# Making a second set of left operands late, in place, instead of storing it and reading it back, and adding two of four kinds of block sums by DMA

## The chip, the core and the metric

The kernel runs on one core of a Trainium2 chip. The engines named in the text are PE (TensorE, the matrix engine; PEld is its weight load), DVE (VectorE), ACT (ScalarE), POOL (GpSimd) and SP (SyncE). In this kernel SP only issues plain DMAs, and POOL issues the other DMAs: the stores and all accumulating ones. All DMAs of the core share 16 DMA engines. The metric is the device time of one execution in microseconds, the median of three runs.

## The reference

With x of 2048 x 512, the reference computes y = g * A + (1 - g) * B, where

- g = sigmoid(sum over d of x * gate_w), one value for a row
- A = Cr @ (x @ Hr^T) - Ci @ (x @ Hi^T): the real part of a two-dimensional Fourier transform, with the matrices Hr, Hi (512 x 512) and Cr, Ci (2048 x 2048) given as inputs
- B = (relu(x @ Wg) * (x @ Wu)) @ Wd, with a hidden width of 1792

```
a = jnp.einsum("bsd,ed->bse", x, dft_hid_re)
b = jnp.einsum("bsd,ed->bse", x, dft_hid_im)
y = jnp.einsum("ts,bse->bte", dft_seq_re, a) - jnp.einsum("ts,bse->bte", dft_seq_im, b)
gate = jnp.einsum("bsd,df->bsf", x, W_gate); up = jnp.einsum("bsd,df->bsf", x, W_up)
b = jnp.einsum("bsf,fd->bsd", gate * (gate > 0) * up, W_down)
return g * a + (1 - g) * b
```

All of it is in float32.

## The kernel before, in words

**Products.** A float32 operand is split into two float32r parts: hi is a copy of it on ACT, lo is operand minus hi on DVE. A product is then three passes over PE: lo*hi, hi*lo, hi*hi. On top of that each matrix product of two by two blocks is done with seven block products instead of eight (Strassen's way, in Winograd's form). Each of the seven needs a left and a right operand that is a block or a sum of blocks. They are numbered 1 to 7; for the stages looked at here they run in the order 1, 5, 6, 3, 7, 2, 4.

**Stages.** In order of time: the blocks of the gated unit (relu and product, the result h goes to DRAM as hd); two spectral parts, which compute x @ Hr^T and x @ Hi^T and store them to DRAM as ad; two more blocks of the gated unit; two Down rounds (h @ Wd; the result goes to vd, its negative to zd); four Sequence rounds, numbered here by (m, p): m = 0 is Cr, m = 1 is Ci, p is one half of the output rows. They run (0,0), (0,1), (1,1), (1,0); the last is of the class `Last`.

**A Sequence round** has 7 products x 4 groups (jj) of 12 matmuls = 336 matmuls of 128 x 128 by 512. The left operands are the spectral result, one set of 14 tiles of 512 KB in hi and lo (28 tiles) for each m; the right ones are blocks "11", "12", "22", "21" of Cr or Ci, 512 KB for each block and jj, loaded by SP into tiles `r`. Sums of blocks are made in place (`rights`, line 850): for product 5, r11 += r12; for 7, r12 += r22; for 6, r11 += r22; for 4, r11 += r21. Before the change all four kinds are DVE additions, four of each in a round. Each right operand is split into `ch` (ACT) and `cl` (DVE), 31 and 24 matmuls ahead of its use by the plan. When a product is done, `evac` takes PSUM out with ACT or DVE, and `done` brings a finished block of the output on its way: with m = 0 it is added to zd by an accumulating DMA.

**Left operands.** The class `Left` (line 700) loads the four blocks of ad as `l`, makes the sums 5, 7, 6 and 3 on DVE, and splits each into `lh` and `ll`. The set of m = 0 is made during Down 1 and round (0,0) and stays in SBUF. The set of m = 1 is made early by `prep` (line 733), one half (n = 0) during the second spectral part and one (n = 1) during Down 0; its 28 tiles are stored to a DRAM tensor `lb` by POOL, and `fetch` (line 746) reads them back with SP during round (0,1), each as soon as the tile of the first set that it replaces is used up.

**The last round.** `Last.prepare` (line 883) runs during (1,1): for all four blocks it loads z from zd and v from vd, makes v + gate * z on DVE and stores it to vd by POOL. In (1,0) the blocks "12" and "22" then take vd by an accumulating DMA (line 894), and "11" and "21" load v again and add the product's two halves on DVE.

**What sets the order.** Nothing is scheduled by hand. Each operation is handed to a planner (`Plan`, line 128) with a key, the number of the matmul beside which it may start. The planner models the durations of all engines and one common line for DMA data, works out how late each operation may be, and writes one fixed order for each engine. ACT and DVE may run up to 40 matmuls ahead of a key, SP and POOL not at all. SBUF is 51 units of 4 KB for each partition; a load or a result waits in the plan until a unit is free, and on the chip until the last user of its unit is done, a storing DMA included. Every engine, SP and POOL too, works through its order strictly in turn. Two constants of the model concern DMAs: the time of its data (line 111) and `LANDING` (line 133).

```
op(key + 18, lambda t=t, m=m, x=x: store(to[m - 1, n, x], f32(t.all)))
for x, (o, i) in {5: ("11", "12"), 7: ("12", "22"), 6: ("11", "22"), 4: ("11", "21")}.items():
    op(at[x, jj] - SUM[x], lambda r=r, o=o, i=i: combine(r[o].all, r[o].all, r[i].all, 1))
op(k + 10, lambda b=b, v=v: store(vd[self.place(b)], v.all))
```

Of the kernel before, what the change touches and what calls it, by code (L numbers as in the profile page):

```python
# [9 lines left out]
F32R = mybir.dt.float32r  # L10
# [4 lines left out]
P = 128  # L15
# [73 lines left out]
class Step:  # L89


    def __init__(self, key, engine, name, a, k):
        self.key, self.engine, self.name, self.a, self.k = key, engine, name, a, k
        refs = [x for x in a if isinstance(x, Ref)]
        refs += [k[x] for x in ("out", "in_") if isinstance(k.get(x), Ref)]
        writes = [k["out"] if "out" in k else a[0]]
        if "accum_out" in k:
            writes.append(k["accum_out"])
        self.writes = [x for x in writes if isinstance(x, Ref)]
        self.reads = [x for x in refs if x is not writes[0]]  # L100
        if "accum_op" in k or name == "matmul" and not k["start"]:
            self.reads += self.writes
        self.after, self.start, self.end, self.due = set(), None, None, None
        n = writes[0].size() if self.writes else 0
        self.hold = None
        if name == "tensor_copy":
            self.work = 0.1 + n * 0.52e-3
            self.hold = self.work - 0.05
        elif name == "dma_start":
            n = max(x.size() // (P if x.base.kind == "dram" else 1) for x in (*self.writes, *self.reads))  # L110
            self.work = n * 4 * P / 4096 * 0.157 / 16 * (2 if "accum_op" in k else 1)
        elif engine == "tensor":
            self.work = self.hold = 0.22667 * n / N
        elif engine == "vector":
            self.work = 0.16 + n * 1.0417e-3
            self.hold = self.work - 0.083
        else:
            self.work = 0.19 + n * 0.845e-3
            self.hold = self.work - 0.09
# [8 lines left out]
class Plan:  # L128
# [1 line left out]

    MATMUL, WAIT, LANDING = 0.22667, 0.035, 2.1

    ISSUE = {"sync": 0.5, "scalar": 0.5, "gpsimd": 0.9}

# [6 lines left out]
    def op(self, key, f, *a):  # L143
        self.ops.append((key, len(self.ops), f, a))
# [133 lines left out]
def kernel(ctx: ExitStack, tc, xP, xG, wf, wgu, wd, cr, ci, wri, gw, out):  # L278
# [27 lines left out]
    def hbm(name, *shape):  # L306
        return Buf(plan, name, shape, kind="dram", tile=dram.tile(list(shape), F32, name=name))
# [1 line left out]
    hd = hbm("hd", 2, 7, P, KF // 2, N)  # L309
    ad = hbm("ad", 2, 2, 2, 2, P, 4, HD)  # L310
    vd, zd = (hbm(n, NT, P, KD, N) for n in ("vd", "zd"))
    lb = hbm("lb", 7, 2, 2, P, 4, HD)
    wb = hbm("wb", 8, P, 4, 2, P)
    gd = hbm("gd", NT * KD, P)
    gwt = Buf(plan, "gwt", [D], kind="fixed", tile=small.tile([P, D], F32, name="gwt"))
# [5 lines left out]
    def buf(name, shape=(2, N), dtype=F32):  # L321
        return Buf(plan, name, list(shape), dtype)
# [21 lines left out]
    def E():  # L344
        return plan
# [4 lines left out]
    def f32(ap):  # L350
        return ap.bitcast(F32)
# [4 lines left out]
    def load(o, i):  # L356
        plan.sync.dma_start(o, i)

    def store(o, i):
        plan.gpsimd.dma_start(out=o, in_=i)  # L360
# [42 lines left out]
    class Weights:  # L403
# [34 lines left out]
        def fetch(self, key):  # L438
            for n, t in enumerate(y for x in (self.a, self.b) for i in x for y in i):
                k = t.shape[0]  # L440
                op(key + 6 * n, lambda n=n, t=t, k=k: load(f32(t.all), wb[n, :, :k]))
# [182 lines left out]
    class Spectral:  # L624
# [8 lines left out]
        def prep(self, m, key):  # L633
            raw = self.raw[{1: "11", 2: "12", 4: "22", 7: "21"}[m]] if m in (1, 2, 4, 7) else buf(f"vs{m}")
            w = self.w[m] = buf(f"vh{m}", dtype=F32R), buf(f"vl{m}", dtype=F32R), raw
            if len(LEFT[m]) > 1:
                a, b = ((self.raw[n] if isinstance(n, str) else self.w[n][2]) for n in LEFT[m][:2])
                op(key, lambda: combine(raw.all, a.all, b.all, LEFT[m][2]))
            op(key + 4, hi_of, w)
            op(key + 8, lo_of, w)  # L640
# [59 lines left out]
    class Left:  # L700
# [29 lines left out]
                op(key, lambda: E().scalar.copy(hi[:, s], raw[:, s]))  # L730
                op(key + step, lambda: E().vector.tensor_sub(lo[:, s], raw[:, s], f32(hi[:, s])))

        def prep(self, n, key, step, to=None):

            for b in BLOCKS:
                op(key - 60, self.load, b, n)
            for m in (1, 5, 7, 6, 2, 3, 4):
                if m in (3, 5, 6, 7):
                    op(key, self.sum, m, n)
                self.split(m, n, key + 4, 8)  # L740
                for x in range(2):
                    t = self.t[m, n][x]
                    op(key + 18, lambda t=t, m=m, x=x: store(to[m - 1, n, x], f32(t.all)))
                key += step

        def fetch(self, m, n, key, of):
            t = self.t[m, n] = [buf(f"lb{m}", [4, HD], F32R) for _ in range(2)]
            for x in range(2):
                op(key, lambda x=x: load(f32(t[x].all), of[m - 1, n, x]))

    SUM = {5: 40, 7: 40, 6: 40, 4: 88}

    class Round:

# [86 lines left out]
    class Sequence(Round):  # L841
        HI, LO = 31, 24

        def __init__(self, left, m, p):
            self.m, self.p = m, p
            if m:
                self.g = gate_row(p, plan.now + 100)
            super().__init__(left, (2, 2, 2, 2))

        def rights(self):  # L850
            at = self.at
            for jj in range(4):
                r = {b: buf(f"r{b}") for b in BLOCKS}
                for b, key in (("11", at[1, jj]), ("12", at[5, jj]), ("22", at[6, jj] - 10), ("21", at[2, jj] - 36)):
                    op(key - 90, lambda r=r, b=b, jj=jj: load(
                        r[b].all, (cr, ci)[self.m][2 * self.p + int(b[1]) - 1, int(b[0]) - 1, jj]))
                for x, (o, i) in {5: ("11", "12"), 7: ("12", "22"), 6: ("11", "22"), 4: ("11", "21")}.items():
                    op(at[x, jj] - SUM[x], lambda r=r, o=o, i=i: combine(r[o].all, r[o].all, r[i].all, 1))
                for x in ORDER_Z:
                    self.split(x, jj, r[{1: "11", 3: "22", 5: "11", 7: "12", 6: "11", 2: "21", 4: "11"}[x]])  # L860

        def place(self, b):
            return 2 * self.p + int(b[1]) - 1, slice(None), slice(2 * int(b[0]) - 2, 2 * int(b[0]))

        def gate(self, b, g=None):
            return (g or self.g)[:, int(b[1]) - 1].unsqueeze(1).to_broadcast([P, 2, N])

        def done(self, b, key):
            o = self.o[b]
# [10 lines left out]
    class Last(Sequence):  # L880


        def prepare(self, key):

            g = gate_row(self.p, key - 60)
            for i, b in enumerate(BLOCKS):
                k, z, v = key + 40 * i, buf("z"), buf("v")
                op(k - 50, lambda b=b, z=z: load(z.all, zd[self.place(b)]))
                op(k - 50, lambda b=b, v=v: load(v.all, vd[self.place(b)]))
                op(k, lambda b=b, z=z: E().vector.tensor_mul(z.all, z.all, self.gate(b, g)))  # L890
                op(k + 2, lambda v=v, z=z: combine(v.all, v.all, z.all, 1))
                op(k + 10, lambda b=b, v=v: store(vd[self.place(b)], v.all))

        def done(self, b, key):
            o = self.o[b]
            op(key, lambda: E().vector.tensor_mul(o.all, o.all, self.gate(b)))
            op(key + 4, lambda: accumulate(o.all, vd[self.place(b)]))
            op(key + 30, lambda: load(out[self.place(b)], o.all))

        def part(self, v, b, n, p, sign):  # L900
            E().vector.tensor_mul(self.o[b][:, n], p[n], self.g[:, 0])
            combine(v[:, n], v[:, n], self.o[b][:, n], sign)

        def middle(self, key):
            v = buf("v")
            op(key - 50, lambda: load(v.all, vd[self.place("11")]))
            for n in range(2):
                op(key, self.part, v, "11", n, PAIRS["x"], 1)
            op(key + 8, lambda: load(out[self.place("11")], v.all))

        def end(self, key):
            v = buf("v")
            t, _, es = self.place("21")

            op(key - 90, lambda: load(v.all, vd[self.place("21")]))
            for n in range(2):
                op(key - 6 + 6 * n, self.part, v, "21", n, PAIRS["t"], -1)
                op(key - 6 + 6 * n, lambda n=n: load(out[t, :, es.start + n], v[:, n]))

# [79 lines left out]
        return Left(source)  # L1001

    lefts = [spectrum(f) for f in range(2)]
    lefts[1].prep(0, plan.now + 72, 14, lb)
    for ih in range(2):
        SpectralBlock(spectral, 1, ih)
    blocks(tail)
# [6 lines left out]
    for n in range(2):  # L1014
# [2 lines left out]
            op(key + k + 6 * n, lw.sum, m, n)  # L1017
        for m, k in ((5, -90), (6, 10), (3, 48), (7, 88), (2, 130), (4, 170)):
            lw.split(m, n, key + k + 14 * n, 8)
    lefts[1].prep(1, key + 130, 22, lb)  # L1020
    Down(lw, 0)
    key = plan.now
    la = lefts[0]
# [9 lines left out]
    for n, (m, p) in enumerate(((0, 0), (0, 1), (1, 1), (1, 0))):  # L1033
        if n == 1:
            start = plan.now
            for i, x in enumerate(ORDER_Z):
                for k in range(2):
                    lefts[1].fetch(x, k, plan.now + 48 * i + 24 * k + 40, lb)
        if n < 3:
            Sequence(lefts[m], m, p)  # L1040
        else:
            Last(lefts[m], m, p).prepare(start + 540)

    plan.run(nc, unit)

# [54 lines left out]
```

## Time and profile before

| | |
|---|---|
| three runs | 806.33, 808.00, 808.09 us; median 808.0 us |
| the profiled execution | 805.16 us, of which 803.4 us from its first to its last instruction |
| PE busy | 791.2 us (98%), 3474 matmuls |
| DVE, ACT, POOL busy | 587.8, 387.5, 92.1 us |
| DMA | 192.78 MB |
| granted PE clock, mean | 0.997 |

A line of a group or of the timeline names what an instruction writes and reads as out<-in, by tile names with numbers left out: `lb<-lh` is the store of a hi left tile to DRAM, `r<-ci` a load of a block of Ci. All instructions have line 125, that of the helper that issues them, so one goes by tile names. The busy time of PE counts a matmul from its issue to its modelled end, and two in flight overlap: one is shown 0.39 us long, while they start some 0.23 us apart.

By the numbers of matmuls, the rounds of this execution lie at 488.8 us for (0,0), 565.0 for (0,1), 641.1 for (1,1) and 721.9 to 798.0 for (1,0); the second spectral part at 275.5 to 317.4, the two blocks after it to 355.5, Down 0 to 422.2, Down 1 to 488.8.

### The profile page before, as it was taken

How to read it: one execution, taken by the hardware profiler on the slowest of the kernel's cores; microseconds unless marked ns; L12 is line 12 of the kernel's file. 1: busy time of each engine (PE TensorE's matmuls, PEld its weight loads, DVE VectorE, ACT ScalarE, POOL GpSimd, SP SyncE). 2: the span in 40 equal slices, each digit the busy share in tenths (PEclk: the TensorE clock that was granted, in tenths of full speed). 3: DMA queues.
4: the chain of work that ended last, by engine and by line, in shares of the span. 5: the costliest groups of instructions: out<-in, count | busy, mean ns of one | idle time of the engine just before them, and what ended most of it. 6: DMA issues, size and time to landing. Idle time of an engine off the chain costs nothing.

```text
span 803.4 us, 9431 instructions
## 1 busy us (share of the span) xinstructions
PE 791.2 (98%) x3474; PEld 653.5 (81%) x3474; DVE 587.8 (73%) x644; ACT 387.5 (48%) x419; POOL 92.1 (11%) x146
## 2 busy tenths in 40 slices
PE   9999999999999998999999999999999999989997
PEld 8888888888888886888888888888888888868885
DVE  7978765656568245897875899885768486889992
ACT  5644342424245345575575688454445343434540
POOL 1002211111202123120220010000000000100000
PEclk9999999999999999999999999999999999999999
DMA  9516534242648589989899998228888966699443
GB/s 332 231 40 217 195 125 145 92 144 92 197 143 287 200 336 417 407 300 347 276 413 408 404 314 315 81 59 251 241 274 284 348 245 210 192 333 339 157 105 105
DMA packets 55182, 192.78 MB, mean 240 GB/s; under 512 B 6368, under 2 KB 6624, under 8 KB 55136
## 3 DMA queue, kind: packets, MB, share of 16 engines
q1 hardware_dynamic: 35840, 121.92, 42.7%
q0 software_dynamic: 19296, 70.26, 25.2%
q8 instruction: 27, 0.44, 0.2%
q14 instruction: 19, 0.16, 0.1%
HBM read 120.85 MB, written 71.31 MB: 239 GB/s over the span
## 4 chain that ended last, share of the span: by engine, by line
PE 83%; issue 10%; DMA 4%; POOL 2%; DVE 1%; ACT 0%; POOLq 0%; ACTq 0%; DVEq 0%
PE ps L125 83%; DMA lb<-lh 1%; DMA vd<-v 1%; DMA ad<-a 1%; POOL ad L125 1%; POOL hd L125 1%; DVE z L125 0%; POOL z L125 0%; DVE h L125 0%; DVE v L125 0%; DVE u L125 0%; DVE cl L125 0%; ACT a L125 0%; ACT ps L125 0%; DVE hs L125 0%
## 5 line engine op out<-in xcount | busy, mean ns | idle before, releaser
L125 DVE TENSOR_TENSOR cl<-r,ch 128x1024 fp32r<-128x1024 f32 x112 | 134.6, 1221 | 45.9 <-ACT ch L125 26.6
L125 ACT CAST ch<-r 128x1024 fp32r<-128x1024 f32 x112 | 114.9, 1051 | 104.2 <-PE ps L125 40.8
L125 PE MATMUL ps<-ch,ll 128*128 128x512 f32 x420 | 163.4, 389 | 0.0
L125 PE MATMUL ps<-cl,lh 128*128 128x512 f32 x420 | 163.4, 389 | 0.0
L125 PE MATMUL ps<-ch,lh 128*128 128x512 f32 x420 | 163.4, 389 | 0.0
L125 PE MATMUL ps<-ch,lb 128*128 128x512 f32 x448 | 139.5, 392 | 0.0
L125 PEld LDWEIGHTS ps<-ch,lb 128*128 128x128 f32 x448 | 84.8, 189 | 17.8
L125 PEld LDWEIGHTS ps<-ch,ll 128*128 128x128 f32 x420 | 78.8, 188 | 16.5
L125 PEld LDWEIGHTS ps<-cl,lh 128*128 128x128 f32 x420 | 78.8, 188 | 16.3
L125 PEld LDWEIGHTS ps<-ch,lh 128*128 128x128 f32 x420 | 78.8, 188 | 16.3
L125 PE MATMUL ps<-cl,lb 128*128 128x512 f32 x224 | 87.9, 392 | 2.7 <-DVE cl L125 2.7
L125 DVE TENSOR_TENSOR r<-r,r 128x1024 f32<-128x1024 f32 x64 | 77.1, 1219 | 3.8 <-DMA r<-cr 2.1
L125 DVE TENSOR_TENSOR cl<-hr,ch 128x1024 fp32r<-128x1024 f32 (+1 forms) x56 | 59.8, 1086 | 20.5 <-ACT ch L125 19.3
L125 ACT COPY s<-ps 128x1024 f32<-128x1024 f32 x42 | 42.6, 1014 | 56.5 <-PE ps L125 54.1
L125 ACT CAST ch<-hr 128x1024 fp32r<-128x1024 f32 (+1 forms) x56 | 51.4, 941 | 25.2 <-DMA hr<-hd 14.1
L125 PEld LDWEIGHTS ps<-cl,lb 128*128 128x128 f32 x224 | 42.5, 190 | 12.1 <-DVE cl L125 3.3
L125 ACT COPY ps<-ps 128x1024 f32<-128x1024 f32 x23 | 23.0, 999 | 59.6 <-PE ps L125 39.6
L125 DVE TENSOR_TENSOR ll<-l,lh 128x1024 fp32r<-128x1024 f32 (+1 forms) x24 | 28.0, 1175 | 24.1 <-ACT lh L125 17.1
L125 ACT ACTIVATE ps<-ps 128x1024 f32<-128x1024 f32 x23 | 23.2, 1007 | 41.4 <-DVE u L125 23.1
L125 DVE TENSOR_TENSOR u<-ps,s 128x1024 f32<-128x1024 f32 x26 | 31.4, 1219 | 15.6 <-PE ps L125 12.9
L125 POOL DMA_DIRECT2D hd<-h x28 | 18.0, 642 | 184.0 <-DVE h L125 184.0
L125 PE MATMUL ps<-vh,xl 128*128 128x512 f32 x88 | 34.6, 393 | 3.2 <-ACT ps L125 2.7
(206 smaller groups left out, 1357.0 us busy)
## 6 DMA issues: line engine op xcount, KB each, us to landing
hr<-hd SPq DMA_DIRECT2D x42, 512.0 KB, 7.7
r<-cr SPq DMA_DIRECT2D x32, 512.0 KB, 5.2
r<-ci SPq DMA_DIRECT2D x32, 512.0 KB, 9.6
hd<-hs POOLq DMA_DIRECT2D x28, 512.0 KB, 5.6
lb<-lb SPq DMA_DIRECT2D x28, 512.0 KB, 5.1
ad<-a POOLq DMA_DIRECT2D x16, 512.0 KB, 8.3
l<-ad SPq DMA_DIRECT2D x16, 512.0 KB, 6.5
wr<-wgu SPq DMA_DIRECT2D x14, 512.0 KB, 7.5
```

Source lines behind the costliest of these rows:

```text
L125: getattr(getattr(nc, self.engine), self.name)(*map(ap, self.a), **{k: ap(x) for k, x in self.k.items()})
```

## The change

`prep`, `fetch` and the DRAM tensor lb go. In their place `late` loads the four blocks of ad during round (0,1), and makes the sums and splits of the second set one product after another, each 88 matmuls ahead of its first use in round (1,1), so in the last third of (0,1) and the first two thirds of (1,1). The sums of kinds 7 and 4 become accumulating DMAs from SBUF to SBUF, issued by POOL, with more time ahead of their use; kinds 5 and 6 stay on DVE. In the last round only the blocks "11" and "21" are prepared, within that round and without going through vd; "12" and "22" go the way of the third round (an accumulating DMA from zd, a load of v, two DVE operations, a store). Two constants of the planner's DMA model become larger, and so all its orders may come out a little different.

```diff
-            self.work = n * 4 * P / 4096 * 0.157 / 16 * (2 if "accum_op" in k else 1)
+            self.work = n * 4 * P / 4096 * 0.175 / 16 * (2 if "accum_op" in k else 1)
...
-    MATMUL, WAIT, LANDING = 0.22667, 0.035, 2.1
+    MATMUL, WAIT, LANDING = 0.22667, 0.035, 2.5
...
-    lb = hbm("lb", 7, 2, 2, P, 4, HD)
...
-        def prep(self, n, key, step, to=None):
...
-        def fetch(self, m, n, key, of):
...
-    SUM = {5: 40, 7: 40, 6: 40, 4: 88}
+        def late(self, key):
+
+            for i, b in enumerate(("11", "21", "22", "12")):
+                for n in range(2):
+                    op(key - 200 + (24 if b == "12" else 8) * i + 4 * n, self.load, b, n)
+            for m, k in ((5, -84), (7, -72), (6, -28), (3, 18)):
+                for n in range(2):
+                    op(key + k + 6 * n, self.sum, m, n)
+            for i, m in enumerate(ORDER_Z):
+                for n in range(2):
+                    self.split(m, n, key + 48 * i - 88 + 12 * n, 8)
+
+    SUM = {5: 40, 6: 40, 7: 170, 4: 140}
...
-                self.g = gate_row(p, plan.now + 100)
+                self.g = gate_row(p, plan.now + (20 if isinstance(self, Last) else 100))
...
-                    op(at[x, jj] - SUM[x], lambda r=r, o=o, i=i: combine(r[o].all, r[o].all, r[i].all, 1))
+                    f = (lambda o, i: accumulate(o, i)) if x in (4, 7) else (lambda o, i: combine(o, o, i, 1))
+                    op(at[x, jj] - SUM[x], lambda f=f, r=r, o=o, i=i: f(r[o].all, r[i].all))
...
     class Last(Sequence):
-        def prepare(self, key):
-
-            g = gate_row(self.p, key - 60)
-            for i, b in enumerate(BLOCKS):
-                k, z, v = key + 40 * i, buf("z"), buf("v")
+        def prepare(self):
+
+            for b, k in (("11", self.base + 110), ("21", self.base + 160)):
+                z, v = buf("z"), self.v[b]
                 op(k - 50, lambda b=b, z=z: load(z.all, zd[self.place(b)]))
                 op(k - 50, lambda b=b, v=v: load(v.all, vd[self.place(b)]))
...
-                op(k + 10, lambda b=b, v=v: store(vd[self.place(b)], v.all))
-
-        def done(self, b, key):
-            o = self.o[b]
-            op(key, lambda: E().vector.tensor_mul(o.all, o.all, self.gate(b)))
-            op(key + 4, lambda: accumulate(o.all, vd[self.place(b)]))
-            op(key + 30, lambda: load(out[self.place(b)], o.all))
...
-    lefts[1].prep(0, plan.now + 72, 14, lb)
...
-    lefts[1].prep(1, key + 130, 22, lb)
...
-            for i, x in enumerate(ORDER_Z):
-                for k in range(2):
-                    lefts[1].fetch(x, k, plan.now + 48 * i + 24 * k + 40, lb)
-        if n < 3:
-            Sequence(lefts[m], m, p)
-        else:
-            Last(lefts[m], m, p).prepare(start + 540)
+            lefts[1].late(start + 336)
+        (Sequence if n < 3 else Last)(lefts[m], m, p)
```

`start` is the first matmul of round (0,1), so the key given to `late` is the first matmul of (1,1).

More of the change, by code (lines that the diff above doesn't have):

```diff
@@ L731, in split @@
                 op(key + step, lambda: E().vector.tensor_sub(lo[:, s], raw[:, s], f32(hi[:, s])))
-        def prep(self, n, key, step, to=None):
[L735 to L744, printed above, removed]
-        def fetch(self, m, n, key, of):
-            t = self.t[m, n] = [buf(f"lb{m}", [4, HD], F32R) for _ in range(2)]
-            for x in range(2):
-                op(key, lambda x=x: load(f32(t[x].all), of[m - 1, n, x]))
-    SUM = {5: 40, 7: 40, 6: 40, 4: 88}
+        def late(self, key):
[9 more added lines that the diff above has]
+    SUM = {5: 40, 6: 40, 7: 170, 4: 140}
     class Round:
@@ L863, in place, with gate @@
             return 2 * self.p + int(b[1]) - 1, slice(None), slice(2 * int(b[0]) - 2, 2 * int(b[0]))
-        def gate(self, b, g=None):
-            return (g or self.g)[:, int(b[1]) - 1].unsqueeze(1).to_broadcast([P, 2, N])
+        def gate(self, b):
+            return self.g[:, int(b[1]) - 1].unsqueeze(1).to_broadcast([P, 2, N])
         def done(self, b, key):
@@ L880 @@
     class Last(Sequence):
-        def prepare(self, key):
-            g = gate_row(self.p, key - 60)
-            for i, b in enumerate(BLOCKS):
-                k, z, v = key + 40 * i, buf("z"), buf("v")
+        def prepare(self):
+            for b, k in (("11", self.base + 110), ("21", self.base + 160)):
+                z, v = buf("z"), self.v[b]
                 op(k - 50, lambda b=b, z=z: load(z.all, zd[self.place(b)]))
                 op(k - 50, lambda b=b, v=v: load(v.all, vd[self.place(b)]))
-                op(k, lambda b=b, z=z: E().vector.tensor_mul(z.all, z.all, self.gate(b, g)))
+                op(k, lambda b=b, z=z: E().vector.tensor_mul(z.all, z.all, self.gate(b)))
@@ L891, in prepare, with rights @@
                 op(k + 2, lambda v=v, z=z: combine(v.all, v.all, z.all, 1))
-                op(k + 10, lambda b=b, v=v: store(vd[self.place(b)], v.all))
-        def done(self, b, key):
-            o = self.o[b]
-            op(key, lambda: E().vector.tensor_mul(o.all, o.all, self.gate(b)))
-            op(key + 4, lambda: accumulate(o.all, vd[self.place(b)]))
-            op(key + 30, lambda: load(out[self.place(b)], o.all))
-        def part(self, v, b, n, p, sign):
+        def rights(self):
+            super().rights()
+            self.v = {b: buf("v") for b in ("11", "21")}
+            self.prepare()
@@ L901, in part @@
+        def part(self, b, n, p, sign):
             E().vector.tensor_mul(self.o[b][:, n], p[n], self.g[:, 0])
-            combine(v[:, n], v[:, n], self.o[b][:, n], sign)
+            combine(self.v[b][:, n], self.v[b][:, n], self.o[b][:, n], sign)
         def middle(self, key):
-            v = buf("v")
-            op(key - 50, lambda: load(v.all, vd[self.place("11")]))
             for n in range(2):
-                op(key, self.part, v, "11", n, PAIRS["x"], 1)
-            op(key + 8, lambda: load(out[self.place("11")], v.all))
+                op(key, self.part, "11", n, PAIRS["x"], 1)
+            op(key + 8, lambda: load(out[self.place("11")], self.v["11"].all))
@@ L911, in end @@
         def end(self, key):
-            v = buf("v")
             t, _, es = self.place("21")
-            op(key - 90, lambda: load(v.all, vd[self.place("21")]))
             for n in range(2):
-                op(key - 6 + 6 * n, self.part, v, "21", n, PAIRS["t"], -1)
-                op(key - 6 + 6 * n, lambda n=n: load(out[t, :, es.start + n], v[:, n]))
+                op(key - 6 + 6 * n, self.part, "21", n, PAIRS["t"], -1)
+                op(key - 6 + 6 * n, lambda n=n: load(out[t, :, es.start + n], self.v["21"][:, n]))
```

## The prediction

> **What bounds the kernel now.** I read the page first, then the waits of PE, then the timeline at each wait.
>
> ```profile
> PE 791.2 (98%) x3474; PEld 653.5 (81%) x3474; DVE 587.8 (73%) x644; ACT 387.5 (48%) x419; POOL 92.1 (11%) x146
> PE ps L125 <- ACT ps L125: 2.7, 2, 2.4
> PE ps L125 <- DVE cl L125: 2.7, 1, 2.7
> PE ps L125 <- DVE gs L125: 1.2, 1, 1.2
> PE ps L125 <- ACT s L125: 0.5, 1, 0.5
> ```
>
> PE is busy from end to end and the change leaves every matmul in place. So nothing is to be won but PE's waits, and nothing lost but by new ones. The waits (sum, times, longest) are 7.1 us; the 1.2 us on `gs` is the start, which stays. The other four lie in two places, at 300 to 314 us (0.3, 0.5, 2.4) and at 715 us (2.7).
>
> ```profile
> 311.39 0.39 PE L125 MATMUL ps<-vl,xh 128*128 128x512 f32 x1
> 311.62 0.39 PE L125 MATMUL ps<-vh,xh 128*128 128x512 f32 x1
> 314.41 0.50 PE L125 MATMUL ps<-vh,xl 128*128 128x512 f32 x1 [2.40 <-ACT ps L125]
> 314.75 0.40 PE L125 MATMUL ps<-vl,xh 128*128 128x512 f32 x1
> ...
> 714.87 0.50 PE L125 MATMUL ps<-cl,lb 128*128 128x512 f32 x1 [2.66 <-DVE cl L125]
> 715.21 0.64 PE L125 MATMUL ps<-ch,lb 128*128 128x512 f32 x2
> ```
>
> A wait costs more than its figure. Matmuls start 0.23 us apart (311.39, 311.62) but are shown 0.39 long, so 0.16 us of each gap is not shown as idle; and the first one after a wait takes 0.34 us to the next start, 0.11 more. That is 0.27 for each wait: first place 3.2 + 3 x 0.27 = 4.0, second 2.66 + 0.27 = 2.9. After the second the clock falls as well:
>
> ```profile
> 716.00:718.00 2.00, 2.00 (x7) 1.53 (x5) 2.00 (x2) 0.00 (x0) 0.56 (x1) 0.50 1.05 272
> 718.00:720.00 2.00, 2.00 (x7) 1.60 (x6) 1.97 (x3) 1.05 (x1) 0.00 (x0) 0.66 1.03 311
> ```
>
> The columns are PE, PEld, DVE, ACT, POOL, then granted clock, DMA share and GB/s. A clock of 0.50 and 0.66 over 2 us each loses 1.0 + 0.7 = 1.7 us. Together: 4.0 + 2.9 + 1.7 = 8.6 us.
>
> [...]
>
> What stands behind the two waits:
>
> ```profile
> 309.88 1.02 ACT L125 COPY a<-ps 128x1024 f32<-128x1024 f32 x1 [3.65 <-DMA lb<-ll]
> 312.40 1.04 ACT L125 CAST lh<-lr 128x1024 fp32r<-128x1024 f32 x1 [1.51 <-DMA lb<-lh]
> 313.35 1.01 ACT L125 ACTIVATE ps<-ps 128x1024 f32<-128x1024 f32 x1
> ...
> 713.59 1.22 DVE L125 TENSOR_TENSOR cl<-r,ch 128x1024 fp32r<-128x1024 f32 x1 [3.30 <-DMA vd<-v]
> ```
>
> ACT sat behind stores to lb, because a tile it was to write lay in a unit that a store was still reading, and so came late to the copy of PSUM that PE waited for. In the same way DVE's split waited for the store vd<-v of `Last.prepare`.
>
> **The change part by part.**
>
> ```profile
> L125 SPq DMA_DIRECT2D lb<-lb x28: 319/326/843, 573.0 to 642.6; - x28
> L125 POOL DMA_DIRECT2D lb<-lh x14: 532/534/580, 294.9 to 420.1; - x14
> ...
> L125 POOL DMA_DIRECT2D vd<-v x4: 550/561/561, 690.8 to 724.3; - x4
> ```
>
> *Early making, stores and loads of lb.* Out go 28 stores (14 of hi as shown, as many of lo) and 28 loads. In the second spectral part ACT and DVE lose a half set: 7 splits each, 4 sums. The first place's waits go with them, -4.0 us. What is late next there is the stores of ad, then the loads of Wd; I take 0. The same again is taken from Down 0, where PE did not wait: 0. On SP the loads of r lose 28 loads ahead of them and get 8 of ad.
>
> *vd<-v in `prepare`.* The four stores go, and with them the second place: -2.9 and -1.7 us.
>
> ```profile
> 488.80:565.00 76.20, 76.20 (x338) 63.10 (x337) 63.04 (x55) 38.42 (x38) 3.67 (x5) 1.00 0.52 158
> 565.00:641.10 76.10, 76.10 (x337) 63.00 (x337) 50.16 (x43) 33.28 (x33) 3.40 (x4) 1.00 0.87 287
> 641.10:721.90 80.80, 78.14 (x338) 63.98 (x337) 62.09 (x54) 33.25 (x34) 5.09 (x7) 0.98 0.74 246
> 721.90:798.00 76.10, 76.10 (x337) 62.84 (x335) 63.54 (x58) 29.69 (x30) 3.14 (x4) 1.00 0.58 186
> ...
> 466.00:512.00 46.00, 46.00 (x204) 38.10 (x203) 46.00 (x42) 34.84 (x36) 4.27 (x8) 1.00 0.68 246
> L125 DVE TENSOR_TENSOR r<-r,r 128x1024 f32<-128x1024 f32 x64 | 77.1, 1219 | 3.8 <-DMA r<-cr 2.1 <-DMA r<-ci 1.7
> ```
>
> *DVE and ACT in the rounds.* Half of the 64 sums leave DVE: 8 x 1.22 = 9.8 us a round. The late set puts 8 sums and 14 splits on it, 22 x 1.22 = 27 us; by the keys 6 sums and 4 splits (12 us) fall into round (0,1), 2 sums and 10 splits (15 us) into (1,1). So DVE has in (0,1) 50 - 10 + 12 = 52 us of 76, in (1,1) 62 - 10 + 15 = 67, less the 5 that two blocks of `prepare` take with them into the last round. Densest are the 240 matmuls (54 us) around the change of these rounds: 20 splits of right sides, 8 sums of them, 8 left sums, 8 left splits, 44 x 1.22 = 54 us. That is full. But before the change DVE was busy for all of 466 to 512 us without one wait of PE, and a left split is due 88 matmuls (20 us) ahead. I take 0, bounded by 0 and, if the queue runs one sum and split late, 2.4 us. ACT's 14 more copies meet 33 us of 76: 0.
>
> *The 32 accumulating DMAs.*
>
> ```profile
> 536.00:540.00 4.00, 4.00 (x19) 3.30 (x19) 4.00 (x4) 1.94 (x2) 0.00 (x0) 1.00 0.84 131
> 696.00:698.00 2.00, 2.00 (x11) 1.65 (x10) 0.49 (x1) 0.01 (x1) 0.00 (x0) 1.00 1.02 418
> q0 software_dynamic: 103, 0.42, 70.2%
> q1 hardware_dynamic: 111, 0.40, 35.7%
> DMA to landing us min/median/max: 3.1/6.7/15.0
> ...
> zd<-z POOLq DMA_DIRECT2D x8, 512.0 KB, 7.9
> L125 POOL DMA_DIRECT2D zd<-z x8: 844/852/881, 534.8 to 642.6; - x8
> ```
>
> The two queue rows are 636 to 639 us, the landing row is that of the tile r (SP's loads).
>
> No row shows one from SBUF to SBUF. The nearest is a lone one to DRAM, 536 to 540 us: 0.52 MB for 0.84 x 4 = 3.4 us of all 16 engines. A plain transfer, the lower end, takes 0.52 / 0.418 = 1.25 us. I take 3.4. Eight in a round are 27 us. With them the DMA engines are asked for 0.52 x 76 + 27 = 67 us in (0,0); 0.87 x 76 + 27 - 35 (28 loads of lb) + 10 (8 of ad) = 68 in (0,1); 0.74 x 81 + 27 - 15 (12 transfers of `prepare`) = 72 in (1,1), and about as much in the last; of 76 each. It fits, and (0,1) stood at 0.87 before without a wait. The sums 7 and 4 stand 139 and 109 matmuls (31 and 25 us) ahead of their splits; with 7 us for the right block to land and 8 for itself, that holds. I take 0. POOL issues for 0.85 us each, 7 us a round beside 3 to 5 busy: 0. Each stands at POOL until its right block has landed; behind it there are only accumulations of finished blocks, for which no engine waits. The new wait that could hurt is ACT's, at the copies of 7 and 4: behind them in ACT's order are the copies of PSUM, and PE waits for those. It begins only if landing takes 10 us more than both medians.
>
> [...]
>
> *The last round.* Blocks "12" and "22" now end with a DVE product and sum and a store; the later one is due 12 matmuls (2.7 us) before the end, beside a DVE that has no splits left. Upper bound 1.25 us, if that store stands ahead of the two final ones; I take 0.
>
> *The planner's constants.* They can move any instruction. Between 20 and 300 us PE had no wait; I take 0, bounded by one wait like those above, +2.9.
>
> Sum: -4.0 - 2.9 - 1.7 = -8.6 us. The profiled execution of 805.16 us would become 796.6; the median of the runs is 2.8 above that execution, so 799.4. For unforeseen short waits I add 1.1: 800.5 us.
>
> **The rivals.**
>
> ```profile
> L125 ACT CAST ch<-r 128x1024 fp32r<-128x1024 f32 x112 | 114.9, 1051 | 104.2 <-PE ps L125 40.8
> ```
>
> *A. Slower: accumulating DMAs starve the loads of the right block "22".* By the q0 and q1 rows, an accumulation beside loads, both queues get as many packets, 103 and 111, so plain loads fall to 0.40 MB in 3 us, 3.9 us for 512 KB instead of 1.25. At the start of a round up to five accumulations (one `done`, four of kind 7) follow each other. The last load of "22" is issued 32 matmuls (7.3 us) into the round. Its sum 6 is used at matmul 132 (29.9 us), less sum, copy and split (1.2 + 1.05 + 1.2 us): it must land within 19 us. Two loads ahead of it and itself make 11.7, and 1.9 for the rest of landing (the least, 3.1, less 1.25), which holds; from two more on, 21 us (outputs and v of the round before, which is what the third and the last round have) DVE stands at the sum, all its later splits stand behind, and PE waits. For it: the landing of 15.0 us already seen, and a DVE that has less to do and so comes to the sum earlier. Against it: DVE's waits on r were 3.8 us in 64 sums, and none reached PE. Price: a wait like that of 715 us, 2.9 + 1.7 = 4.6 us. One leaves a gain of 4.0 (805), two take it all, three, one in each later round, give 808 - 8.6 + 13.8 = 813.
>
> *B. One place stays.* The wait at 715 us turns up behind another DMA, such as the store of out or the accumulation that the unit's last user now is: 800.5 + 4.6 = 805.
>
> *C. No change.* ACT comes late at 300 to 314 us all the same, behind the stores of ad, and one new wait takes the second place: 808. Against it: the three waits of ACT there name lb twice over, and without the early set there is nothing on ACT to wait for a unit but results of PE.
>
> **How the numbers follow.** Forecast (both places go, 798 to 804): 0.50. One wait of A's kind or B, 804 to 805.5: 0.14. C, and A with two waits, 805.6 to 810.4: 0.08. A from three waits on: 0.28, half of it above 813. A measurement of this kernel tells 0.3% (2.4 us) from no change. So faster 0.64, same 0.08, slower 0.28. The likeliest case's own range is 798 to 804; to hold 8 in 10 it reaches into A, to 813.
>
> **What would show it.** Right: no wait of PE between the start and the end but short ones, no clock row under 1.0, no tile lb; DMA share near 0.9 in all rounds; r<-r as 32 DVE sums, 32 DMAs r<-r with 3.4 us of the engines. Wrong: DVE or ACT idle behind DMA r<-ci, r<-cr or r<-r with PE waiting on cl or ch just after a round begins (A); a wait behind a store (B); waits of ACT near 300 us (C). An accumulation within SBUF dearer than 3.4 us, or DVE's full stretch around 641 us, would break the sum first.

## The result and the profile after

The kernel after takes 796.89 us (796.05 to 797.27), the kernel before, beside it, 808.05 us (806.33 to 808.69). The ratio is 0.9864 with a 95% interval of 0.9847 to 0.9881: 11 us less. Faster was the right side, but 796.9 lies below the range of 798 to 813. The profiled execution of after takes 796.05 us, 794.3 of them from first to last instruction, against 805.16 and 803.4 of before.

First lines of the page of after (span, busy times, the shares of its chain), then the one wait of PE that is left:

```profile
span 794.3 us, 9282 instructions
...
PE 787.9 (99%) x3474; PEld 652.3 (82%) x3474; DVE 550.1 (69%) x610; ACT 387.2 (49%) x419; POOL 101.7 (13%) x146
...
PE 99%; DVE 0%; issue 0%
```

```profile
PE ps L125 <- DVE gs L125: 1.2, 1, 1.2
```

Nothing is left of the four waits: the 1.2 us are the start. From 2 us to the end no two matmuls start more than 0.34 us apart, and the chain is PE to 99%, where it was 83% before. In the stretch where PE had waited for ACT, the timeline of ACT of after now reads:

```profile
299.48 1.03 ACT L125 ACTIVATE s<-ps 128x1024 f32<-128x1024 f32 x1 [1.72 <-PE ps L125]
302.24 1.01 ACT L125 COPY s<-ps 128x1024 f32<-128x1024 f32 x1 [1.74 <-PE ps L125]
304.92 1.01 ACT L125 COPY a<-ps 128x1024 f32<-128x1024 f32 x1 [1.66 <-PE ps L125]
...
307.64 1.01 ACT L125 ACTIVATE ps<-ps 128x1024 f32<-128x1024 f32 x1 [0.76 <-PE ps L125]
```

The roles are changed over: ACT waits for PE, not for a store, and is there when a product ends. The four Sequence rounds of after (columns as before: PE, PEld, DVE, ACT, POOL, clock, DMA share, GB/s):

```profile
484.60:560.70 76.10, 76.10 (x338) 63.00 (x337) 51.17 (x44) 38.25 (x39) 10.38 (x13) 1.00 0.80 207
560.70:636.80 76.10, 76.10 (x337) 63.03 (x336) 54.43 (x48) 38.92 (x41) 10.23 (x12) 1.00 0.94 255
636.80:713.00 76.20, 76.20 (x338) 63.08 (x337) 61.68 (x53) 41.38 (x42) 10.22 (x12) 1.00 0.81 210
713.00:788.90 75.90, 75.90 (x336) 62.67 (x334) 55.05 (x50) 28.95 (x29) 9.35 (x11) 1.00 0.83 234
```

DVE has 54 and 62 us in the second and third round, where the prediction had 52 and 62 to 67. The DMA engines are at 0.80, 0.94, 0.81, 0.83, where it had 0.88, 0.89, 0.95 and about the same. The accumulations within SBUF are a little cheaper than the 3.4 us that the prediction took for one. From 642 to 652 us nothing but accumulations moved, up to 644.3 us one to DRAM among them, after that those within SBUF alone:

```profile
DMA packets 580, 2.11 MB, mean 211 GB/s; under 512 B 64, under 2 KB 64, under 8 KB 580
...
q0 software_dynamic: 580, 2.11, 106.9%
```

That is 512 KB in 2.5 us when they follow each other (211 GB/s from 645 to 652 us as well; four land at 646.7, 649.2, 651.7 and 654.2 us), against 1.25 us for a plain transfer at the 418 GB/s that the prediction shows for 696 to 698 us of before.

### The profile page after: what moved, and what is told of

It reads as the page before. It is cut to its first block, busy times and chain, and to the rows that moved or that the text cites. A ratio compares the mean times of both kernels' runs of the same rounds, so it can differ in the third digit from the quotient of the medians.

```text
span 794.3 us, 9282 instructions
## 1 busy us (share of the span) xinstructions
PE 787.9 (99%) x3474; PEld 652.3 (82%) x3474; DVE 550.1 (69%) x610; ACT 387.2 (49%) x419; POOL 101.7 (13%) x146
## 4 chain that ended last, share of the span: by engine, by line
PE 99%; DVE 0%; issue 0%
PE ps L125 99%; DVE v L125 0%; DVE z L125 0%; DVE warm L125 0%; DVE gs L125 0%
## 5 line engine op out<-in xcount | busy, mean ns | idle before, releaser
L125 PE MATMUL ps<-ch,ll 128*128 128x512 f32 x644 | 250.5, 389 | 0.0
L125 PE MATMUL ps<-cl,lh 128*128 128x512 f32 x644 | 250.5, 389 | 0.0
L125 PE MATMUL ps<-ch,lh 128*128 128x512 f32 x644 | 250.5, 389 | 0.0
L125 PEld LDWEIGHTS ps<-ch,lh 128*128 128x128 f32 x644 | 120.9, 188 | 25.2
L125 PEld LDWEIGHTS ps<-cl,lh 128*128 128x128 f32 x644 | 120.9, 188 | 25.1
L125 PEld LDWEIGHTS ps<-ch,ll 128*128 128x128 f32 x644 | 120.9, 188 | 25.0
L125 DVE TENSOR_TENSOR r<-r,r 128x1024 f32<-128x1024 f32 x32 | 38.6, 1220 | 5.9 <-DMA r<-ci 3.4
L125 PE MATMUL ps<-xh,wb0l 128*128 128x512 f32 x92 | 35.9, 390 | 0.0
L125 PE MATMUL ps<-xl,wb0h 128*128 128x512 f32 x92 | 35.8, 389 | 0.0
L125 PE MATMUL ps<-xh,wb1h 128*128 128x512 f32 x92 | 35.8, 389 | 0.0
```

Of the source, the lines that this page charges most:

```text
L125: getattr(getattr(nc, self.engine), self.name)(*map(ap, self.a), **{k: ap(x) for k, x in self.k.items()})
```

## The experiments

The theory tested is that of the prediction: the gain is PE's waits at two places, near 300 us behind the stores to lb and from 705 us on behind the stores vd<-v. What had to be explained besides is the size: 11.2 us between the medians, of which the waits of the profiled execution are 8.6. Rivals: the constants of the planner, the sums by DMA, and a part of before that the profile did not show.

**The kernel before once more (e0).** No edit.

> The kernel before, unchanged, so that each of its runs is listed with its granted clock. Theory (the gain is the waits at two places, and the second costs more in most runs than in the one execution that was profiled, because the half clock after it lasts longer): 806 to 809 us, mean clock of the runs 0.993 to 0.995 where the profiled execution had 0.997 (each 0.001 is 0.8 us), and a new profile shows the same two places. Rival (the 2 us come from elsewhere, such as the first 10 us): runs at 0.997 as in the profile, times still 806 to 809.

Measured: 807.4 us, 12 runs from 804.9 to 808.8, 17 runs beside them from 804.3 to 809.4. The runs' mean clock lies between 0.995 and 1.000, so the theory's 0.993 to 0.995 is wrong, and the rival's constant 0.997 as well. What the new profile shows is more than both. Its execution took 807.79 us. The waits of PE, and those of DVE at its splits `cl` from 690 us on:

```profile
PE ps L125 <- DVE cl L125: 4.1, 4, 1.7
PE ps L125 <- ACT ps L125: 2.7, 2, 2.5
PE ps L125 <- DVE gs L125: 1.2, 1, 1.2
...
DVE cl L125 <- DMA vd<-v: 2.1, 1, 2.1
DVE cl L125 <- DMA out<-z: 1.7, 1, 1.7
DVE cl L125 <- ACT z L125: 1.4, 1, 1.4
```

The second place is not one wait at 715 us. Here PE waits for DVE four times, at 715, 727, 737 and 755 us, and gaps between matmul starts show three shorter ones; without a fall of the clock there (the granted clock is 1.00 in the stretches 704 to 720, 720 to 740 and 740 to 760 us). The clock falls after the first place instead:

```profile
313.97 0.50 PE L125 MATMUL ps<-vh,xl 128*128 128x512 f32 x1 [2.54 <-ACT ps L125]
314.30 0.40 PE L125 MATMUL ps<-vl,xh 128*128 128x512 f32 x1
...
315.27 0.63 PE L125 MATMUL ps<-vl,xh 128*128 128x512 f32 x1
315.70 0.63 PE L125 MATMUL ps<-vh,xh 128*128 128x512 f32 x1
316.12 0.63 PE L125 MATMUL ps<-vh,xl 128*128 128x512 f32 x1
```

From 314.85 to 318 us the matmuls start 0.43 us apart instead of 0.23, some eight of them: 1.6 us. So the same instructions wait at other points in the two executions, and one profile holds one sample of them.

What all this costs can be added up: of each gap between matmul starts that is longer than 0.3 us, take off the usual 0.23 us. The first place then costs 4.0 us in the first profile and 5.2 in the second, the second place 4.6 and 6.0. Together that is 8.6 against 11.2 us, and the 2.6 us between them are what the second execution took longer (807.79 against 805.16).

**The new last round alone (e1).**

```diff
# kernel before with the class Last of after
-            Last(lefts[m], m, p).prepare(start + 540)
+            Last(lefts[m], m, p)
```

> The kernel before with the new last round alone: no stores vd<-v, the second left set still stored in lb and read back, all sums on DVE. Theory: the wait at 715 us and its half clock go, the one near 300 us stays: 4.6 us less by the profile, up to 7 less by the runs, so 801 to 803.5, clock 0.999. Rival (DVE's load or the planner's constants make the gain): within 1 us of 808, a wait of PE on DVE cl still near 715 us.

Measured: 801.62 us, ratio 0.9926 (0.9907 to 0.9946), 5.6 us less. PE's waits:

```profile
PE ps L125 <- ACT ps L125: 2.3, 1, 2.3
PE ps L125 <- DVE gs L125: 1.2, 1, 1.2
PE ps L125 <- ACT s L125: 0.2, 1, 0.2
```

No wait on cl is left, the first place stands. By the medians the second place costs 5.6 us; the interval, 4.4 to 7.5 us, holds the 4.6 of the first profile too. The six runs lie in two groups: 798.9 and 799.0 us, with a mean clock of 1.000, and four from 801.6 to 801.7, with 0.997 or 0.998. The profile is of the first group. That the other four also lose a fall of the clock, as one of 1.6 us followed the first place in the second profile of before, fits their clock but is not shown.

**The late left set alone (e3).**

```diff
# kernel before with `late` in place of prep, lb and fetch
-    lefts[1].prep(0, plan.now + 72, 14, lb)
...
-    lefts[1].prep(1, key + 130, 22, lb)
...
-                    lefts[1].fetch(x, k, plan.now + 48 * i + 24 * k + 40, lb)
+            lefts[1].late(start + 336)
```

> The kernel before with the late left set alone (all four sums on DVE, the old last round with its stores vd<-v, old constants). Theory: PE's waits near 300 us go (-4.0 us), those near 715 us stay with their half clock: 803 to 805, if DVE, which keeps its 8 sums a round more, holds out; rival (the late set needs the sums off DVE): new waits of PE on cl or ll around 641 us, 806 or more.

Measured: 803.05 us, ratio 0.9958 (0.9942 to 0.9974), 4.1 us less. PE's waits:

```profile
PE ps L125 <- DVE cl L125: 4.2, 3, 2.7
PE ps L125 <- DVE gs L125: 1.2, 1, 1.2
PE ps L125 <- ACT ch L125: 0.2, 1, 0.2
```

The first place is gone, the second is there, with its longest waits at 713, 723 and 738 us, and there is none around 637 us, where the late set is made. The two parts together are 9.7 us of the 10.4 and 11.2 that the whole change brought between the medians of its two comparisons. Some 0.5 us of the rest is time outside of the span from first to last instruction: 802.78 - 800.5 = 2.3 us here, 807.79 - 806.0 = 1.8 in before.

**The stores vd<-v left out**, in the kernel before (e9).

```diff
-                op(k + 10, lambda b=b, v=v: store(vd[self.place(b)], v.all))
```

> The kernel before without the four stores vd<-v of the last round's preparation; gate * z is so left out of its output, all other work is done, DVE's too. Theory (the stores hold the units that DVE's splits need): the waits from 705 to 755 us go, 801 to 803. Rival (DVE is simply full there): they stay, 806 to 808.

Measured: 801.15 us, ratio 0.9928 (0.9911 to 0.9945), as much as the whole new last round. The profile: PE's waits, then 720 to 760 us by stretches, first of this run, then of before (first profile).

```profile
PE ps L125 <- ACT ps L125: 2.4, 1, 2.4
PE ps L125 <- DVE gs L125: 1.2, 1, 1.2
PE ps L125 <- ACT s L125: 0.8, 1, 0.8
```

```profile
720.00:740.00 20.00, 20.00 (x90) 16.58 (x89) 20.00 (x19) 8.66 (x9) 0.84 (x1) 1.00 0.74 269
740.00:760.00 20.00, 20.00 (x90) 16.57 (x89) 19.91 (x18) 12.52 (x14) 0.00 (x0) 1.00 0.48 158
```

```profile
720.00:740.00 20.00, 20.00 (x90) 16.52 (x88) 19.60 (x18) 8.27 (x8) 1.43 (x2) 1.00 1.03 385
740.00:760.00 20.00, 20.00 (x90) 16.57 (x89) 19.96 (x18) 11.76 (x12) 0.00 (x0) 1.00 0.54 177
```

DVE is busy for nearly the whole of 720 to 760 us, as before, and PE waits nowhere after the first place. So DVE's load alone does not make the second place; the stores, which hold units for 8.5 us (the median of the four from issue to landing in before), are needed for it. Once DVE has lost some microseconds to a store (3.3 us in the first profile of before, 2.1 in the second) it has hardly any idle time for 40 us to make them up (of 720 to 760 us 0.4 in the first profile, and in the second 3.6, all of it waits for ACT and for DMAs), and PE waits further on for whatever comes late next: so the series of waits is read here. Two things stay open. Without the stores the planner also writes another order for DVE from 690 us on (up to there it is the same), so a part of the gain can be the order's. And in the second profile of before DVE stood 1.7 us behind the store out<-z, which the change keeps; in this run and in after none of DVE's splits there waits for it.

**The planner's constants alone (e2).**

```diff
-            self.work = n * 4 * P / 4096 * 0.157 / 16 * (2 if "accum_op" in k else 1)
+            self.work = n * 4 * P / 4096 * 0.175 / 16 * (2 if "accum_op" in k else 1)
-    MATMUL, WAIT, LANDING = 0.22667, 0.035, 2.1
+    MATMUL, WAIT, LANDING = 0.22667, 0.035, 2.5
```

> The kernel before with only the two constants of the planner's DMA model changed (0.175, 2.5). Theory: the orders move a little, the stores that hold units stay: 808 within 2 us, waits at both places in some form. Rival (the constants bring the gain): 797 to 801, no waits near 300 and 715 us.

Measured: 802.4 us, ratio 0.9945 (0.9927 to 0.9962), 4.8 us less: neither the 808 of the theory nor the 797 to 801 of the rival. PE's waits, and a line of ACT's timeline:

```profile
PE ps L125 <- DVE cl L125: 4.0, 5, 1.7
PE ps L125 <- DVE gs L125: 1.2, 1, 1.2
...
314.88 1.02 ACT L125 COPY a<-ps 128x1024 f32<-128x1024 f32 x1 [2.64 <-DMA lb<-ll]
```

ACT still stands behind a store to lb for 2.6 us, but the order has changed so that what follows it is a copy for which no product waits. The first place is gone though its stores are not: it takes a store and an order that puts a copy for PE behind it. The second place remains as four waits from 724 to 749 us; a fifth, at 441 us in Down 1, is new.

**The kernel after with the old constants (e5).** The same four lines the other way round.

> The kernel after with the two old constants (0.157, 2.1). Theory (the stores that hold units are gone, so the order hardly matters): 796 to 798, no or one short wait of PE. Rival (the constants were needed, as they alone took 5 us from the kernel before): 800 or more, waits of PE behind DMA r<-cr, r<-ci or r<-r.

Measured: 796.84 us, ratio 0.9866 (0.9852 to 0.9881). With the stores gone the constants are worth nothing that the runs tell apart. The profile, of the slowest of the four runs, has one wait more, at the start:

```profile
PE ps L125 <- ACT wf0h L125: 1.4, 1, 1.4
PE ps L125 <- DVE gs L125: 1.2, 1, 1.2
```

**Sums of kinds 7 and 4 by DMA alone (e4).**

```diff
# kernel before, with SUM = {5: 40, 6: 40, 7: 170, 4: 140}
-                    op(at[x, jj] - SUM[x], lambda r=r, o=o, i=i: combine(r[o].all, r[o].all, r[i].all, 1))
+                    f = (lambda o, i: accumulate(o, i)) if x in (4, 7) else (lambda o, i: combine(o, o, i, 1))
+                    op(at[x, jj] - SUM[x], lambda f=f, r=r, o=o, i=i: f(r[o].all, r[i].all))
```

> The kernel before with the sums of kinds 7 and 4 by DMA alone (lb, the stores vd<-v and the old constants stay). Theory (the gain comes from the late set and the new last round; the sums by DMA take load from DVE but win nothing by themselves near 300 us): the waits near 300 us stay, those from 705 to 755 us shrink or stay, 803 to 808. Rival A of the prediction (accumulations starve the loads of the right blocks): more waits after each round begins, 809 or more.

Measured: 807.47 us, ratio 0.9994 (0.9978 to 1.0010): no change. The waits near 300 us are there, and one on cl of 4.1 us at 727.

**All sums on DVE, in the kernel after (e6).**

```diff
-                    f = (lambda o, i: accumulate(o, i)) if x in (4, 7) else (lambda o, i: combine(o, o, i, 1))
+                    f = lambda o, i: combine(o, o, i, 1)
```

with the old leads of 40, 40, 40 and 88.

> The kernel after with all four kinds of sums on DVE at the old leads. DVE gets 9.8 us a round back: about 64 us of 76 in the second round and 71 in the third. Theory: 797 to 799, as DVE stood full for 46 us before without a wait. Rival (the sums by DMA are what lets the late set in): PE waits on cl or ll from 600 to 700 us, 801 or more.

Measured: 796.17 us, ratio 0.9858 (0.9842 to 0.9875). Its third round:

```profile
636.80:713.00 76.20, 76.20 (x338) 63.10 (x337) 69.54 (x61) 41.44 (x41) 3.41 (x4) 1.00 0.51 153
```

DVE at 69.5 of 76.2 us, the DMA engines at 0.51 instead of 0.81, and no wait of PE either way. The sums by DMA are not what lets the late set in. Whether they cost something was asked by running both kernels once more side by side (a2 is after, e10 all sums on DVE).

> The kernel after, unchanged, beside the next one. Theory: 796 to 797.5 in every run, since there is no wait left that could come out longer or shorter; what scatter remains is the start.

> The kernel after with all four kinds of sums on DVE, once more, beside the kernel after. Theory (sums by DMA and on DVE are both hidden): within 0.1% of it, 796 to 797.2. Rival (the accumulations cost something of their own): 0.5 us or more under it in the medians, with no overlap of the runs.

Measured: after 796.72 us (796.14 to 796.93), all sums on DVE 796.24 us (795.95 to 796.72). The runs overlap, so the 0.5 us are not told apart; if the accumulations make a difference, they cost. Both profiles have slower matmul starts in the first 40 us, at different points, 0.9 us in after and 0.6 with all sums on DVE. Both kernels scatter by 0.8 us in four runs, where the 11 runs of before beside them scatter by 2.9.

**A third kind by DMA (e7).** Kind 6 too, asked 74 matmuls ahead.

```diff
-                    f = (lambda o, i: accumulate(o, i)) if x in (4, 7) else (lambda o, i: combine(o, o, i, 1))
+                    f = (lambda o, i: accumulate(o, i)) if x in (4, 6, 7) else (lambda o, i: combine(o, o, i, 1))
```

> The kernel after with kind 6 by DMA too (12 accumulations a round, kind 6 asked 74 matmuls ahead of its use). The DMA engines, at 0.94 of the second round and 0.8 of the others, get 4 x 2.4 to 3.4 us = 10 to 14 us more a round: 1.07 or more in the second. Theory with rival A's mechanism (plain loads fall to a third beside accumulations): DMA share at 1.0, ACT waits on DMA r<-r, PE waits of some us, 799 to 815. Against it (what is late is still early enough): 796 to 798, no waits.

Measured: 858.51 us, with 12 waits of PE on cl of up to 13.5 us. It says nothing on contention: at that lead the sum stands ahead of product 5's lo part in the program's order (matmul 22 of the round against 24), so that lo part is taken of the block after the sum, and DVE has to wait for the accumulation. That changes the computation, and its time is that of a dependence that was put in.

**The burst of accumulations doubled (e8).** So the contention was asked for by itself:

```diff
+                    if x == 7:
+                        at7 = hd[self.m, jj, :, 2 * self.p:2 * self.p + 2]
+                        op(at[x, jj] - SUM[x], lambda r=r, at7=at7: accumulate(at7, r["22"].all))
```

> The kernel after with 16 accumulating DMAs more: right after each sum of kind 7 the block 22 is also added to a part of hd that nobody reads any more. Nothing waits for them, but eight accumulations instead of four follow each other at the start of each round, 11 us more of the DMA engines in a round. Rival A of the prediction: loads of right blocks land late, DVE and ACT wait for DMA r<-cr and r<-ci, PE behind them, 801 or more. Theory (the right blocks have so much time that a doubled burst is still hidden): 796 to 799.

Measured: 798.40 us (797.39 to 799.91), ratio 0.9898 (0.9882 to 0.9913) to before, 1.7 us above after. First the second and fourth round, then the landing of SP's loads into r, then DVE's and PE's timeline where the one wait is, and last DVE's timeline at the same sum in the kernel after:

```profile
560.70:636.80 76.10, 76.10 (x338) 63.00 (x337) 52.41 (x46) 37.91 (x39) 13.77 (x16) 1.00 1.02 278
...
713.00:788.90 75.90, 75.44 (x333) 62.06 (x332) 54.12 (x49) 29.02 (x29) 12.96 (x15) 1.00 0.95 265
```

```profile
DMA to landing us min/median/max: 3.1/7.2/19.7
```

```profile
739.18 1.23 DVE L125 TENSOR_TENSOR r<-r,r 128x1024 f32<-128x1024 f32 x1 [4.99 <-DMA r<-ci]
```

```profile
743.87 0.50 PE L125 MATMUL ps<-cl,lh 128*128 128x512 f32 x1 [0.47 <-DVE cl L125]
```

```profile
737.72 1.23 DVE L125 TENSOR_TENSOR r<-r,r 128x1024 f32<-128x1024 f32 x1 [3.38 <-DMA r<-ci]
738.87 4.62 DVE L125 TENSOR_TENSOR cl<-r,ch 128x1024 fp32r<-128x1024 f32 x4
```

That is rival A's mechanism: 26 us into the last round DVE stands at a sum for a load of Ci, for 5.0 us, and 5 us later PE waits for a split. The change itself already brings the first half of this about: in after DVE stands at the same sum for 3.4 us. The load behind it takes 8.9 us to land with all sums on DVE (e6), 16.8 in after and 17.9 here. The third split after the sum ends at 742.36 us in after and the matmul that takes it starts at 742.90: 0.5 us to spare, where e6 has 3.3 (0.7 and 3.3 in the profiles a2 and e10 of the same two kernels). Twice the burst uses that up and costs PE 0.5 us in this execution. The median is 1.7 us above after; this is the fastest of the five runs, and where the others lose more is not recorded.

## Why the prediction was right in its direction and missed in its size

*Both places go.* Right, each for the cause that was named: e3 takes the first away (4.1 us measured, 4.0 predicted), e9 and e1 the second (6.0 and 5.6 us measured, 2.9 + 1.7 = 4.6 predicted). What these runs do not separate is the planner's order, which changes with each edit and by e2 can lift the first place by itself.

*The second place's price.* Right for the execution that was profiled, 4.6 us by its matmul starts too. But it was read as one wait and one fall of the clock that every execution has. The second profile shows a stretch of 40 us in which PE waits now here, now there, and there it costs 6.0 us.

*From the profiled execution to the median.* This is the step that failed. "The median of the runs is 2.8 above that execution, so 799.4": the 2.8 us were carried over as if they were something fixed around the span. They were waits too, of the same two places, of which the profiled execution had fewer than most: in the second profile of before the two places cost 11.2 us and not 8.6, and its time is longer by just these 2.6 us. After the change the gap between the median and the profiled execution is 796.89 - 796.05 = 0.8 us. Taken between the two profiled executions the sum was good: -8.6 predicted, 796.05 - 805.16 = -9.1 measured, and of the missing 0.5 us the first matmuls make 0.4: in before four of them took 1.46 us from 5.19 us on, in after 1.08. With 0.8 in place of 2.8 us the forecast would have been 798.5, and a range that reaches as far below it as the stated one, to 796.0, would hold the result.

*"For unforeseen short waits I add 1.1."* There were none; the range's lower end of 798 then excluded the result.

*DVE in the rounds.* Right at 0, with the load as worked out, and right even with 9.8 us more a round (e6). The densest stretch is as full as was said: DVE is busy for 51.6 us of the 54.4 from 609.7 to 664.1 us, and no matmul waits for a split.

*The 32 accumulating DMAs.* Right at 0 on PE's path, but with 0.5 us to spare at one split of the last round, for which the prediction had worked out more room (rival A, below): luck had a part in it. The price was 2.5 us in a burst (211 GB/s in after) to 2.7 (196 GB/s from 642 to 652 us with the burst doubled, e8) where 3.4 was taken from a lone one, which includes its slow first packets (from 536 us of before, 12 of the first 16 took 0.87 to 1.16 us, the median of all 128 of 4 KB 0.33). At either price PE's sum is left alone by the change; with the burst doubled it no longer is.

*The planner's constants.* Taken as 0, with a bound above only. Alone they took 4.8 us off the kernel before, by putting another instruction of ACT behind the store. A bound below was not excluded by any reason and should have stood there. In the kernel after they are worth nothing (e5).

*Rival A* had 0.28. Its mechanism is real and sits where it was put, in the last round at sum 6. In after it holds DVE for 3.4 us and stops short of PE; the load lands after 16.8 us, where the prediction had 13.6 (11.7 + 1.9) against a limit of 19. It reaches PE with twice the accumulations, for 0.5 us in the profiled execution and 1.7 in the median, not 4.6: there is one wait, and the clock does not fall (1.00 from 713.0 to 788.9 us). *Rival B* and *rival C* did not come up.

## What to carry to other kernels

In the kernel before, a tile that was stored from SBUF was occupied until its store had landed (by the medians, 8.5 us after the issue for vd<-v, 10.9 and 11.4 for lb), and an engine that was to write the same memory stood there (ACT for 3.65 us behind lb, DVE for 3.30 behind vd) with everything queued behind it; stores of results that are read back later are the first thing to look for when an in-order engine that feeds the bound one has a wait on a DMA. A kernel with such waits has no single profile (here 8.6 and 11.2 us of waits in two executions): compare the spread of its runs with the waits of the one that was profiled, and take a gap between the two for waits that may go as well. Moving work from an engine that is full but not waited for to DMAs (here 9.8 us a round of DVE) brought nothing, and the DMAs took their time from other loads: the slack of one split fell from 3.3 to 0.5 us.

## What the runs showed of the hardware that was not expected

The fall to about half clock (0.50 granted from 716 to 718 us of the first profile of before) does not follow from the length of the wait alone. Gaps between matmul starts of 2.79 us (314 us, first profile of before), 2.81 us (315 us, without the stores vd<-v) and 3.10 us (713 us, with the late set alone) left the clock at full: the next start came 0.33 or 0.34 us later, those after it 0.22 to 0.24 us apart. Gaps of 2.76 us (314 us, with two kinds of sums by DMA alone, e4), 2.93 us (314 us, second profile of before) and 3.05 us (715 us, first profile) were followed by matmuls 0.43 us apart, for 3.0 us in the second profile and 3.4 in the first; in e4 the rows from 315.1 to 316.8 us show it. What decides between gaps of like length is not shown.

The accumulating DMAs moved their 4 KB packets at half the rate of the plain ones, within SBUF as to DRAM (211 GB/s from 645 to 652 us of after and 197 from 612 to 614 us of before, against 418 from 696 to 698 us of before). The longest landing of SP's loads into r was 10.0 us with all sums on DVE (e6), 16.8 in after, and 19.7 with the burst doubled.
